# A build-time scheduler that charges DMA transposes and casting loads differently (sliding-window attention, then a multiplicative FFN)

## The chip, the cores and the metric

One core of one Trainium2 chip. The metric is device time in microseconds (us) of one execution; lower is better. The time of a kernel is the median of its runs.

## The reference, cut to what matters

```python
B, H, S, D = 4, 8, 768, 64          # q, k, v: float32
scores = matmul(q, k.T) / sqrt(D)
keep   = (key < 4) | ((0 <= row - key) & (row - key < 128))
a      = softmax(where(keep, scores, -1e9))
x      = (a @ v), heads side by side   # 3072 tokens x 512
h      = (x @ w1) * (x @ w2)           # 3072 x 1024
out    = (h @ w3) @ w_out              # 3072 x 512, float32
```

## The kernel before, in words

The work is done for four batches b = 0 to 3, each in two chunks c of 384 tokens. `w3 @ w_out` is folded into one matrix w3o at the start (transposes at L274, products at L299). For a batch, the keys and queries are loaded with a cast from float32 to bfloat16 (L152, issued by GpSimd, POOL), then brought into the transposed layout `qkT`. Batches 0 and 1 do that with TensorE (PE) transposes; batches 2 and 3 with **DMA transposes** issued by SyncE (SP) at L390, twelve for each batch: one for each of six blocks of 128 tokens and each of k and q. There are two homes of `qkT`; batch 2 reuses that of batch 0 and batch 3 that of batch 1.

Attention: scores at L467 (six visits of PE for a batch from batch 1 on), exp at L478 (ACT), masking at L484 (VectorE, DVE), the sink scores at L425 with their exp at L430, and the product with v at L536, normalized at L546 and L551 into `xs`. `xs` is transposed into `xT`, by PE at L572 and DVE at L576 for batches 0 and 1, by SP's DMA transposes at L592 for batches 2 and 3 (three for each chunk). The FFN takes a chunk of `xT`: 64 gate matmuls (L615), copies and products (L622, L630), then three output blocks of 8 matmuls each (L645), a copy (L652) and a store to `out` from SP (L658). A gate needs nothing but `xT` and weights, so FFN work of a chunk that is ready can fill PE while attention waits.

**What sets the order.** Every piece of work is an `Op` with an engine, a duration, the ops it depends on, a priority and the ring slots that it takes and frees. While the program is built, a planner simulates the engines: at each step it takes, over all engines, the op that starts earliest, emits its instructions and sets `o.done`, the time at which its readers may start. On PE, ACT, DVE and SP it takes the op that can start soonest; among those that can start at once, the lowest priority number (attention of batch b has 10b and some, the FFN 1000 and more). POOL takes its ops in the listed order. The planner's times exist only while the program is built; what remains is the order of instructions on each engine. On the chip an engine works through its instructions in that order, and one that waits for its data holds back all behind it.

Loads are charged to one shared DMA order `dma["at"]`: each adds its bytes over a rate and is due `LAND` after its turn. The transposes of L390 and L592 are charged 0.1 us of SP and are due 2.2 us later; the stores of L658 0.1 us and 2.0 us. None of these three touches the shared DMA order. The chunk's three `xT` transposes wait in the plan for one another (`evs[-1:]`).

```python
op.dma = nbytes * (1 + 96.0 / run) / 4.35e5
tp_of[s, kb] = Op(SP, 0.1, dmt, [got[n, b, kb]] + war, base, lat=2.2)
```

Of the kernel before, what the change touches and what calls it, by code (L numbers as in the profile page):

```python
# [21 lines left out]
def kernel(  # L22
# [23 lines left out]
    NP = H // 2  # L46
# [36 lines left out]
    for b in (2, 3):  # L83
        o = (b - 2) * 2 * NQ
# [35 lines left out]

    HOP = 0.12
    LAND = 1.9
    ops = []

    class Op:
# [21 lines left out]
    dma = dict(at=1.6)  # L147
# [41 lines left out]
    got = {}  # L189
# [138 lines left out]
    for b in range(B):  # L328
        kind = 0 if b == 0 else 1
        T = qkT_home[b % 2]  # L330
        war = []
# [50 lines left out]
        if b < 2:  # L382
            tdep = lambda c, r: [tp_of[c, r]] + ([tp_of[0, r]] if c else [])
        else:
            for kb in range(NB):
                for s, n, src in ((0, "k", kN), (1, "q", qN)):
                    got[n, b, kb] = load_nat(src, k if n == "k" else q, b, kb, fold_done)

                    def dmt(b=b, s=s, src=src, kb=kb, T=T):
                        nc.sync.dma_start_transpose(out=T[:, :, s, kb * P:(kb + 1) * P], in_=src[b][:, kb, :])  # L390
                    tp_of[s, kb] = Op(SP, 0.1, dmt, [got[n, b, kb]] + war, base, lat=2.2)
                got["v", b, kb] = load_v(b, kb)
            tdep = lambda c, r: [tp_of[s, kb] for s in range(2) for kb in range(3 * c + 3)]

# [165 lines left out]
        for c in range(NC):  # L560
            holder = [None]
            if b < 2:
                evs = []
                for n_h in range(2):
                    x = [holder]

                    def xtp(c=c, n_h=n_h, x=x, xs_first=xs_first):
                        tp = transposed(x[1].slot["mm"], 6 * P).rearrange("p (r j m) -> p r j m", r=2, m=P)
                        for i in range(2):
                            r = 2 * n_h + i  # L570
                            for j in range(QC):
                                nc.tensor.transpose(tp[:, i, j, :],  # L572
                                                    xs_first[c].slot["xs"][:, j, r * P:(r + 1) * P], ident[:])

                    def xtc(n_h=n_h, x=x):
                        nc.vector.tensor_copy(x[0][0].slot["xT"][:, 2 * n_h:2 * n_h + 2, :],  # L576
                                              transposed(x[1].slot["mm"], 6 * P).rearrange("p (r m) -> p r m", r=2))
                    a = Op(PE, cols(P, 6), xtp, [norm[c, 2 * n_h], norm[c, 2 * n_h + 1]], base + 2.5, takes=["mm"],
                           frees=[(xs_first[c], "xs")] if n_h else [])
                    x.append(a)  # L580
                    ev = Op(DVE, dve_us(6 * P, 2), xtc, [a] + ([holder[0]] if n_h else []), base + 2.5,
                            takes=["xT"] if n_h == 0 else [], frees=[(a, "mm")])
                    if n_h == 0:
                        holder[0] = ev
                    else:
                        a.deps.append(evs[0].deps[0])
                    evs.append(ev)
            else:
                evs = []
                for j in range(QC):  # L590
                    def xtd(c=c, j=j, holder=holder, xs_first=xs_first):
                        nc.sync.dma_start_transpose(out=holder[0].slot["xT"][:, :, j * P:(j + 1) * P],  # L592
                                                    in_=xs_first[c].slot["xs"][:, j, :])
                    ev = Op(SP, 0.1, xtd, [norm[c, r] for r in range(NP)] + evs[-1:], base + 2.5,
                            takes=["xT"] if j == 0 else [], lat=2.2,
                            frees=[(xs_first[c], "xs")] if j == QC - 1 else [])
                    if j == 0:
                        holder[0] = ev
                    evs.append(ev)
            chunk_dep[b, c] = (holder, evs)  # L600

    proj_ops = {}
    for b in range(B):
        for c in range(NC):
            holder, evs = chunk_dep[b, c]
            abh = [None]
            b_ops = []
            for dt in range(KFF):
                pr = 1000 + 200 * b + 100 * c + dt
                x = [holder]  # L610
                deps = evs + got["w", dt // 2]

                def gate(w_sb, dt, pg, holder=holder):
                    for kk in range(NP):
                        nc.tensor.matmul(pg[:, 0:TOK], w_sb[:, kk, dt * P:(dt + 1) * P],  # L615
                                         holder[0].slot["xT"][:, kk, :], start=(kk == 0), stop=(kk == NP - 1))
                y = []
                g1 = Op(PE, cols(TOK, 4), lambda g=gate, dt=dt, y=y: g(w1_sb, dt, y[0].slot["mm"]), deps, pr, takes=["mm"])
                y.append(g1)

                def acopy(y=y):
                    nc.scalar.copy(y[1].slot["a"][:], y[0].slot["mm"][:, 0:TOK])  # L622
                ac = Op(ACT, act_us(TOK), acopy, [g1], 0, takes=["a"], frees=[(g1, "mm")])
                y.append(ac)
                g2 = Op(PE, cols(TOK, 4), lambda g=gate, dt=dt, y=y: g(w2_sb, dt, y[2].slot["mm"]), deps + [g1], pr - 0.5,
                        takes=["mm"], frees=[(holder, "xT")] if dt == KFF - 1 else [])
                y.append(g2)

                def amul(dt=dt, y=y, abh=abh):
                    nc.vector.tensor_mul(abh[0].slot["ab"][:, dt, :], y[1].slot["a"][:], y[2].slot["mm"][:, 0:TOK])  # L630
                am_ = Op(DVE, dve_us(TOK), amul, [g2, ac] + ([abh[0]] if dt else []), 0, takes=["ab"] if dt == 0 else [],
                         frees=[(g2, "mm"), (ac, "a")])
                if dt == 0:
                    abh[0] = am_
                b_ops.append(am_)
            for mi in range(QC):
                m = QC * c + mi
                x = []
                last = b == B - 1 and m == NB - 1
                for n0, n1 in ([(0, 256), (256, 512)] if last else [(0, 512)]):  # L640
                    x = []

                    def proj(mi=mi, n0=n0, n1=n1, abh=abh, x=x):
                        for kk in range(KFF):
                            nc.tensor.matmul(x[0].slot["mm"][:, 0:n1 - n0], abh[0].slot["ab"][:, kk, mi * P:(mi + 1) * P],  # L645
                                             w3o[:, kk, n0:n1], start=(kk == 0), stop=(kk == KFF - 1))
                    p_ = Op(PE, cols(n1 - n0, 8), proj, b_ops + fold_done, 1150 + 200 * b + 100 * c + mi, takes=["mm"],
                            frees=[(abh, "ab")] if mi == QC - 1 and n1 == 512 else [])
                    x.append(p_)

                    def pcopy(n0=n0, n1=n1, x=x):
                        nc.scalar.copy(x[1].slot["o"][:, n0:n1], x[0].slot["mm"][:, 0:n1 - n0])  # L652
                    pc = Op(ACT, act_us(n1 - n0), pcopy, [p_], 0, takes=["o"], frees=[(p_, "mm")])
                    x.append(pc)

                    def pout(b=b, m=m, n0=n0, n1=n1, x=x):
                        t0 = b * S + m * P
                        nc.sync.dma_start(out=out[t0:t0 + P, n0:n1], in_=x[1].slot["o"][:, n0:n1])  # L658
                    Op(SP, 0.1, pout, [pc], 0, frees=[(pc, "o")], lat=2.0)


    free = {PE: 1.0, ACT: 2.2, DVE: 0.9, POOL: 0.9, SP: 0.8}
# [38 lines left out]
        return None if pick_ is None else (pick_[1], pick_[2])  # L701

    with tc.manual_schedule():
        left = len(ops)
        while left:
            moves = []
            for e in free:
                got_ = best(e)
                if got_:
                    moves.append((got_[0], e, got_[1]))  # L710
            start, e, o = min(moves, key=lambda x: (x[0], x[1]))
            if e == PE and start < 24.0 and start - free[PE] > 0.15:
                n = min(24, int((start - free[PE] - 0.1) / (cols(P) * (2 if free[PE] < WARM else 1))))
                sc = sc_home[0] if rings["sc"].free[0] == 0.0 else None
# [13 lines left out]
            us = o.us * (2 if e == PE and start < WARM else 1)  # L728
            free[e] = start + us
            o.done = start + us + o.lat  # L730
            if hasattr(o, "dma"):
                dma["at"] = max(dma["at"], start + us + (0.1 if e == POOL else 0.6)) + o.dma
                o.done = dma["at"] + LAND
            for h, n in o.frees:
                h = h[0] if isinstance(h, list) else h
                key = n
                ring = n[0] if isinstance(n, tuple) else n
                rings[ring].free[h.slot["#", key]] = o.done
# [37 lines left out]
```

## Time and profile before

| what | us |
|---|---|
| runs of the kernel | 231.79, 232.09, 232.44; median 232.09 |
| the profiled execution's own time | 231.57 |
| its span in the profile | 229.9 |
| PE busy in the span | 201.4 (88%) |
| DVE, ACT, POOL busy | 107.1, 100.2, 71.4 |
| PE's first instruction, end of its last | 1.06, 226.7 |

The span runs from the first instruction of the profiled execution to the last; its own time is 1.67 us longer. Busy time of PE counts a matmul for as long as it runs, so that matmuls at half the clock count double. "Idle before" in a row is the time for which the engine had nothing to run just ahead of that instruction, and the name behind the arrow is what ended it. SPq is the queue of SyncE, where DMA issues stand.

### The profile page before, as it was taken

To read this page: it belongs to the slowest core of one execution; us is meant where nothing else is said; L and a number is where in the kernel's file an instruction comes from. 1 tells how busy PE (TensorE), PEld (TensorE's weight loads), DVE (VectorE), ACT (ScalarE), POOL (GpSimd) and SP (SyncE) were. 2 spreads that over 40 slices of the span, in tenths; PEclk is the share of its full clock that TensorE was granted. 3 is DMA by queue.
4 is the path that set the end of the run, shared out by engine and by line. 5 is a ranking of instruction groups with operands and counts; after the bars stand their busy time and mean duration, and the time that the engine had idled before them with its cause. 6 is when DMAs were issued, how large, how long until landed. Compare 5 with 4: busy or idle time off the path is not lost.

```text
span 229.9 us, 4653 instructions
## 1 busy us (share of the span) xinstructions
PE 201.4 (88%) x1880; PEld 125.0 (54%) x1880; DVE 107.1 (47%) x249; ACT 100.2 (44%) x172; POOL 71.4 (31%) x93
## 2 busy tenths in 40 slices
PE   8999799968889953893089999999999999999994
PEld 8886465546546622362046656656555545546543
DVE  2424784568878852154037864773431312403300
ACT  3035554852377731375017667623323424334232
POOL 7846756699993556640000000000000000000000
PEclk9999999999999997589569999999999999999998
DMA  7999999999999999999910025203415012021033
GB/s 142 182 191 185 200 194 177 178 155 152 148 131 122 151 132 156 155 158 156 197 49 4 0 87 151 41 28 119 64 32 174 3 46 91 0 94 46 1 137 137
DMA packets 98437, 26.25 MB, mean 114 GB/s; under 512 B 88944, under 2 KB 94320, under 8 KB 98416
## 3 DMA queue, kind: packets, MB, share of 16 engines
q0 software_dynamic: 74944, 14.42, 81.0%
q1 hardware_dynamic: 23472, 11.54, 24.1%
q8 instruction: 14, 0.23, 0.4%
q14 instruction: 7, 0.06, 0.1%
HBM read 29.36 MB, written 6.29 MB: 155 GB/s over the span
## 4 chain that ended last, share of the span: by engine, by line
PE 55%; DMA 33%; POOL 6%; issue 2%; SPq 1%; ACT 0%; POOLq 0%; ACTq 0%
PE mm L615 30%; PE mm L645 17%; DMA qkT<-big 8%; DMA big<-in_k_dram 6%; DMA big<-in_moe_w_dram 5%; DMA early<-in_k_dram 5%; DMA w_sb<-in_moe_w_dram 4%; PE av L536 4%; DMA big<-in_moe_w_out_dram 3%; DMA vN<-in_v_dram 3%; PE sc L467 3%; POOL near L152 3%; POOL vN L152 1%; POOL big L152 1%; POOL w_sb L152 1%
## 5 line engine op out<-in xcount | busy, mean ns | idle before, releaser
L615 PE MATMUL mm<-xT,w_sb 128*128 128x384 bf16 x512 | 90.8, 329 | 0.1
L615 PEld LDWEIGHTS <-w_sb 128*128 128x128 bf16 x512 | 48.2, 98 | 35.0 <-issue 4.0
L630 DVE TENSOR_TENSOR ab<-a_sb,mm 128x384 bf16<-128x384 f32 x64 | 35.4, 553 | 60.4 <-PE mm L615 55.4
L478 ACT ACTIVATE ex<-sc 128x768 bf16<-128x768 f32 (+2 forms) x52 | 44.5, 896 | 16.6 <-PE sc L467 10.7
L622 ACT COPY a_sb<-mm 128x384 f32<-128x384 f32 x64 | 30.3, 480 | 37.1 <-PE mm L615 20.0
L645 PE MATMUL mm<-w3o,ab 128*128 128x512 bf16 (+1 forms) x200 | 46.3, 387 | 0.0
L645 PEld LDWEIGHTS <-ab 128*128 128x128 bf16 x200 | 19.5, 100 | 22.1 <-issue 3.4
L484 DVE TENSOR_TENSOR am<-ex,maskt 128x768 bf16<-128x768 bf16 (+2 forms) x52 | 30.2, 588 | 2.3 <-ACT ex L478 2.2
L652 ACT COPY o_sb<-mm 128x512 f32<-128x512 f32 (+1 forms) x25 | 14.2, 568 | 33.1 <-PE mm L645 33.1
L152 POOL DMA_DIRECT2D vN<-in_v_dram x24 | 21.2, 884 | 13.2 <-DMA big<-in_k_dram 8.2
L536 PEld LDWEIGHTS <-am 128*128 128x128 bf16 x352 | 18.2, 101 | 4.0 <-issue 1.0
L536 PE MATMUL av<-vN,am 128*128 128x65 bf16 x352 | 19.8, 198 | 0.0
L551 DVE TENSOR_TENSOR xs<-av,rec 128x384 bf16<-128x384 f32 x32 | 17.6, 551 | 0.2
L467 PE MATMUL sc<-qkT 64*128 64x256 bf16 (+1 forms) x248 | 15.0, 248 | 2.8 <-DMA qkT<-big 2.8
L299 PE MATMUL mm<-big,w3t 128*128 128x128 bf16 (+2 forms) x128 | 15.8, 273 | 0.6 <-DMA big<-in_moe_w_out_dram 0.6
L425 PE MATMUL mm<-qkT,ksbd 128*32 128x512 bf16 (+2 forms) x20 | 2.2, 432 | 15.3 <-DMA qkT<-big 14.7
L546 DVE RECIPROCAL rec<-av 128x6 f32<-128x6 f32 x32 | 6.2, 193 | 19.3 <-PE av L536 19.0
L303 ACT CAST w3o<-mm 128x128 bf16<-128x128 f32 (+2 forms) x16 | 5.9, 372 | 17.8 <-PE mm L299 17.7
L536 PE MATMUL av<-vsb,es 128*128 128x130 bf16 x64 | 13.5, 227 | 0.0
L467 PEld LDWEIGHTS <-qkT 64*128 64x128 bf16 x248 | 8.5, 97 | 8.6 <-issue 7.3
L299 PEld LDWEIGHTS <-w3t 128*128 128x128 bf16 x128 | 9.5, 98 | 4.5 <-issue 0.7
L152 POOL DMA_DIRECT2D big<-in_q_dram x12 | 10.6, 881 | 4.1 <-DMA vN<-in_v_dram 4.1
(52 smaller groups left out, 130.9 us busy)
## 6 DMA issues: line engine op xcount, KB each, us to landing
out_dram<-o_sb SPq DMA_DIRECT2D x23, 256.0 KB, 2.0
vN<-in_v_dram POOLq DMA_DIRECT2D x24, 128.0 KB, 10.1
w_sb<-in_moe_w_dram POOLq DMA_DIRECT2D x8, 256.0 KB, 9.7
big<-in_moe_w_dram POOLq DMA_DIRECT2D x7, 256.0 KB, 7.9
big<-in_k_dram POOLq DMA_DIRECT2D x12, 128.0 KB, 11.4
big<-in_q_dram POOLq DMA_DIRECT2D x12, 128.0 KB, 11.1
near<-in_k_dram POOLq DMA_DIRECT2D x6, 128.0 KB, 7.2
near<-in_q_dram POOLq DMA_DIRECT2D x6, 128.0 KB, 6.8
```

What stands on the lines that cost most here:

```text
L152: op = Op(eng, us, lambda: (nc.gpsimd if eng == POOL else nc.sync).dma_start(out=out, in_=in_), deps)
L299: nc.tensor.matmul(po, x[1].slot["w3t"][:, j, :], wo_sb[:, j, c0:c1], start=(j == 0), stop=(j == KFF - 1))
L467: nc.tensor.matmul(sc[:, e, c * P:(c + n) * P], T[hp, r, 0, kb * P:(kb + 1) * P], T[hp, r, 1, qb * P:(qb + n) * P], start=True, stop=True)
L478: nc.scalar.activation(y[1].slot["ex"][:, :, 0:w], y[0].slot["sc", i][:, :, 0:w], ACTF.Exp, scale=scale)
L484: nc.vector.tensor_mul(y[2].slot["am"][:, :, 0:w], y[1].slot["ex"][:, :, 0:w], maskt[:, :, m0:m0 + w].to_broadcast([P, 2, w]))
L536: nc.tensor.matmul(o, lhs, rhs, start=(i == 0), stop=(i == len(todo) - 1), skip_group_check=True)
L551: nc.vector.tensor_mul(xs_first[c].slot["xs"][:, :, r * P:(r + 1) * P].rearrange("p k (e d) -> p k e d", d=D), x[0].slot["av"][:, :, :, 0: ...
L615: nc.tensor.matmul(pg[:, 0:TOK], w_sb[:, kk, dt * P:(dt + 1) * P], holder[0].slot["xT"][:, kk, :], start=(kk == 0), stop=(kk == NP - 1))
L622: nc.scalar.copy(y[1].slot["a"][:], y[0].slot["mm"][:, 0:TOK])
L630: nc.vector.tensor_mul(abh[0].slot["ab"][:, dt, :], y[1].slot["a"][:], y[2].slot["mm"][:, 0:TOK])
L645: nc.tensor.matmul(x[0].slot["mm"][:, 0:n1 - n0], abh[0].slot["ab"][:, kk, mi * P:(mi + 1) * P], w3o[:, kk, n0:n1], start=(kk == 0), stop= ...
L652: nc.scalar.copy(x[1].slot["o"][:, n0:n1], x[0].slot["mm"][:, 0:n1 - n0])
```

## The change

The planner gets other costs; no op and no instruction is added or removed. A DMA transpose takes `TUS` = 1.25 us of SP, and its `turn`, also 1.25 us, of the shared DMA order. It is due 0.6 us after its start, plus its turn (twice that if the shared order is busy then), plus 1.3 us. A store keeps 0.1 us of SP and gets a turn of 0.7 us by the same formula. A POOL load may start only when the eighth load before it is due.

```diff
+    TUS = 1.25
...
-                    tp_of[s, kb] = Op(SP, 0.1, dmt, [got[n, b, kb]] + war, base, lat=2.2)
+                    tp_of[s, kb] = Op(SP, TUS, dmt, [got[n, b, kb]] + war, base)
+                    tp_of[s, kb].turn = TUS
...
-                    ev = Op(SP, 0.1, xtd, [norm[c, r] for r in range(NP)] + evs[-1:], base + 2.5,
-                            takes=["xT"] if j == 0 else [], lat=2.2,
+                    ev = Op(SP, TUS, xtd, [norm[c, r] for r in range(NP)] + evs[-1:], base + 2.5,
+                            takes=["xT"] if j == 0 else [],
                             frees=[(xs_first[c], "xs")] if j == QC - 1 else [])
+                    ev.turn = TUS
...
-                    Op(SP, 0.1, pout, [pc], 0, frees=[(pc, "o")], lat=2.0)
+                    Op(SP, 0.1, pout, [pc], 0, frees=[(pc, "o")]).turn = 0.7 * (n1 - n0) / 512
...
-        left = len(ops)
+        left, lanes = len(ops), []
...
             start, e, o = min(moves, key=lambda x: (x[0], x[1]))
+            if e == POOL and hasattr(o, "dma"):
+                if len(lanes) >= 8 and lanes[-8] > start:
+                    free[POOL] = lanes[-8]
+                    continue
...
             o.done = start + us + o.lat
+            if hasattr(o, "turn"):
+                busy = dma["at"] > start + 0.6
+                dma["at"] = max(dma["at"], start + 0.6) + o.turn
+                o.done = start + 0.6 + o.turn * (2 if busy else 1) + 1.3
             if hasattr(o, "dma"):
                 dma["at"] = max(dma["at"], start + us + (0.1 if e == POOL else 0.6)) + o.dma
                 o.done = dma["at"] + LAND
+                if e == POOL:
+                    lanes.append(o.done)
```

## Rows read from the trace of the kernel before

**Rows 1.** The page: busy shares, then PE, its clock and DMA in 40 slices.
```profile
PE 201.4 (88%) x1880; PEld 125.0 (54%) x1880; DVE 107.1 (47%) x249; ACT 100.2 (44%) x172; POOL 71.4 (31%) x93
...
PE   8999799968889953893089999999999999999994
...
PEclk9999999999999997589569999999999999999998
DMA  7999999999999999999910025203415012021033
```

**Rows 2.** Waits of PE, 80 to 120 us: who waited for whom, total us, times, longest.
```profile
PE mm L425 <- DMA qkT<-big: 14.7, 2, 10.4
PE sc L467 <- DMA qkT<-big: 2.8, 1, 2.8
```

**Rows 3.** Timeline of PE, 81 to 132 us: start, us, what, idle before.
```profile
81.13 0.39 PE L467 MATMUL sc<-qkT 64*128 64x256 bf16 x6
84.33 0.34 PE L467 MATMUL sc<-qkT 64*128 64x256 bf16 x4 [2.80 <-DMA qkT<-big]
84.60 2.89 PE L645 MATMUL mm<-w3o,ab 128*128 128x512 bf16 x8
...
92.79 0.62 PE L425 MATMUL mm<-qkT,ksbd 128*32 128x512 bf16 x4 [4.32 <-DMA qkT<-big]
...
115.81 0.62 PE L425 MATMUL mm<-qkT,ksbd 128*32 128x512 bf16 x4 [10.40 <-DMA qkT<-big]
...
131.87 1.90 PE L645 MATMUL mm<-w3o,ab 128*128 128x512 bf16 x8
```

**Rows 4.** PE by stretches: stretch, us, busy (count), granted clock, DMA share, GB/s.
```profile
84.33:88.47 4.14, 4.14 (x27) 0.62 1.92 155
92.79:98.40 5.61, 5.61 (x35) 0.50 1.89 156
98.40:101.00 2.60, 2.60 (x22) 0.88 1.98 153
115.81:119.90 4.09, 4.09 (x31) 0.55 0.00 0
120.00:160.00 40.00, 40.00 (x417) 1.00 0.20 56
```

**Rows 5.** The chain that ended last, 75 to 116 us: start, us, what.
```profile
75.56 8.73 DMA qkT<-big
...
85.72 6.94 DMA qkT<-big
...
98.13 12.98 DMA big<-in_k_dram
...
112.45 3.27 DMA qkT<-big
```

**Rows 6.** Timeline of PE, the end of the run.
```profile
160.34 9.26 PE L615 MATMUL mm<-xT,w_sb 128*128 128x384 bf16 x56
169.43 5.34 PE L645 MATMUL mm<-w3o,ab 128*128 128x512 bf16 x24
174.61 10.56 PE L615 MATMUL mm<-xT,w_sb 128*128 128x384 bf16 x64
```

**Rows 7.** The transposes of L390: ns min/median/max on SP's queue.
```profile
L390 SPq DMA_TRANSPOSE qkT<-big x24: 1188/1236/3111, 62.3 to 112.4; - x24
```

**Rows 8.** DMA issues: KB each (none given for transposes), median us to landing.
```profile
out_dram<-o_sb SPq DMA_DIRECT2D x23, 256.0 KB, 2.0
...
big<-in_k_dram POOLq DMA_DIRECT2D x12, 128.0 KB, 11.4
...
qkT<-big SPq DMA_TRANSPOSE x24, 7.2
...
xT<-xs SPq DMA_TRANSPOSE x12, 2.5
```

**Rows 9.** Timeline of POOL: first and last load for batches 2 and 3 (36 in all).
```profile
55.58 0.88 POOL L152 DMA_DIRECT2D big<-in_k_dram  x1
...
101.28 0.87 POOL L152 DMA_DIRECT2D vN<-in_v_dram  x1 [0.82 <-DMA big<-in_k_dram]
```

**Rows 10.** Timeline of SP's queue, 62 to 138 us.
```profile
62.33 36.58 SPq L390 DMA_TRANSPOSE qkT<-big  x18
99.00 0.53 SPq L658 DMA_DIRECT2D out_dram<-o_sb  x1
101.13 6.75 SPq L390 DMA_TRANSPOSE qkT<-big  x3
107.98 0.53 SPq L658 DMA_DIRECT2D out_dram<-o_sb  x1
108.60 5.06 SPq L390 DMA_TRANSPOSE qkT<-big  x3
113.76 21.34 SPq L658 DMA_DIRECT2D out_dram<-o_sb  x2
135.34 1.19 SPq L592 DMA_TRANSPOSE xT<-xs  x1
```

**Rows 11.** Timeline of DVE: last mask of batch 1, sink keys, last `xT` copies of batch 1.
```profile
82.25 0.68 DVE L484 TENSOR_TENSOR am<-ex,maskt 128x1024 bf16<-128x1024 bf16 x1
82.85 0.34 DVE L398 COPY ksbd<-qkT 64x16 bf16<-64x16 bf16 x2
...
101.49 0.56 DVE L576 COPY xT<-mm 128x768 bf16<-128x768 bf16 x1 [1.90 <-PE mm L572]
...
105.44 0.56 DVE L576 COPY xT<-mm 128x768 bf16<-128x768 bf16 x1 [0.31 <-PE mm L572]
```

## The prediction

> **What bounds the kernel now.** I began with the page's slices [rows 1]. PE is busy 201.4 us and every other engine about half of that or less, so PE is the bound, except where its row dips. The early dips and the last slice belong to the start and the final store. The dips that matter are in slices 15, 16 and 19 to 21 (80 to 92 us and 103 to 121 us), where the DMA row still reads 9 until loading ends near 115 us. Next I asked who PE waits for between 80 and 120 us: three waits, all for `qkT<-big`, the DMA transposes of batches 2 and 3, 14.7 + 2.8 = 17.5 us together [rows 2]. The timeline places them: 2.80 us in the middle of batch 2's first scores, 4.32 us at batch 2's sink scores, 10.40 us at batch 3's sink scores [rows 3]. The chain agrees: at these points it runs through transposes landing at 84.3, 92.7 and 115.7, and through the load ahead of the last of them [rows 5].
>
> The waits cost more than their length. After each of them PE works at 1.2 GHz for a while: granted 0.62, 0.50, 0.88 and 0.55 of full in the four stretches of work [rows 4]. A granted share g over t us means 2(1-g)t us at the lower level: 3.15 + 5.61 + 0.62 + 3.68 = 13.1 us. It can be seen in one instruction group: eight output matmuls take 2.89 us at 84.60 and 1.90 us at 131.87 [rows 3]. At full clock these 13.1 us of work take half, so 6.5 us are lost. From 120 to 160 us PE is busy throughout at 1.00 [rows 4]. So the recoverable sum is 17.5 + 6.5 = 24.0 us.
>
> Is there work to put there? Batch 1's two chunks of FFN are nearly all still to come at 105 us, and batch 0's output blocks too: the second half of `xT` for batch 1 is copied only at 101.49 and 105.44 [rows 11], because the last products of batch 1's attention stand in PE's order behind batch 2's scores and so behind the waits. The order is the fault, not a lack of work.
>
> **The change, part by part.** No instruction is added, so only the order can change. I work the code's formulas through POOL's and SP's lists; this tells when the planner believes data to be there, hence what stands ahead of what, and not what the chip will need.
>
> *Up to 58 us of the planner's time nothing moves.* POOL's list is fixed, and the limit of eight moves only issues: eight loads of batch 2 or 3 are 8 x 131072 x 2 x 1.375 / 435000 = 6.6 us of the shared order, more than the 2.9 us of issue and landing, so that order stays full and every due time as it was. The limit alone costs and brings nothing; it makes loads take their turn in the order among the transposes. The trace supports eight in flight: 36 loads start between 55.58 and 101.28, one in 1.31 us, and land 11.4 us after issue, 8.7 of them at a time [rows 8, 9].
>
> *The transposes of L390.* Charged now with 1.25 us of SP; the trace shows a median of 1.236 us on the queue [rows 7]. Landing is charged 3.15 us, or 4.4 behind a busy order, against a measured 7.2 and 3.27 us after the loads [rows 5, 8]. Three loads and two transposes then take 2.5 + 2.5 us of the order. Batch 2's last transpose is due at 84.0 instead of 74.0, batch 3's at 113.6 instead of 89.0. Measured: 92.7 and 115.7 [rows 5]. The new belief is 9 us too early for batch 2, and 2 us for batch 3.
>
> *Where PE then stands.* By its own costs the planner of before reached batch 2's scores at 77.2; the trace has them at 81.13 [rows 3], a lag of 3.9 us. In place of those scores PE now gets batch 0's three output blocks, 5.2 us [rows 6], and some 2 us of the last products and transposes of batch 1, which brings it to about 88.4 on the chip and past 84.0 in the plan. Then batch 2 comes again: one visit of scores whose transposes are there, a gate or none, then the sink scores or the next visit, which wait for the transpose landing at 92.7. I put PE there at 89.3, so **3.5 us of the batch 2 wait stay**; bounds 0 (several gates placed ahead) and 7.1 (both present waits). I add half a clock's loss after it: 6.2 us at the lower level were seen behind the 4.32 us wait (5.61 + 0.62), so 3.1 us; bounds 0 and 4.
>
> *Batch 3.* Planned from 113.7 on, on the chip 113.7 + 3.9 + 3.5 + 3.1 = 124, against transposes that landed at 115.7 [rows 5]. Between 84 and 113.7 the plan needs 30 us of work and has 2 x 15.6 of gates and output blocks for batch 1, 5.2 for batch 0's second chunk [rows 6] and some 7.5 of batch 2's attention, 44 us. So **the 10.40 us go, with the 3.7 us at the lower clock behind them**, and some 14 us are left to fill batch 3's attention. What is late next is SP's queue: six stores of batch 0 and batch 2's first `xT` transposes will stand among batch 3's last transposes, and each waits for PE. By the plan batch 3's last transpose starts at 109.2; with PE's lag of 10.5 us SP may reach it only at 119.7, and it lands 3.3 us later, at 123, one us before PE comes. Should that cover fail, the cost is the overshoot and a clock loss (rival B). The stores' bytes move into the time of loading, 0.7 us each by the plan and 0.53 us on the queue [rows 10]; 3 us more of DMA before batch 3's last landing, 119, is still ahead of 124.
>
> *The `xT` transposes and the stores.* `xT` is charged 3.15 to 4.4 us where 2.5 is measured [rows 8], in a chain of three, so batch 2's gates are planned up to 6 us late; the 14 us of batch 1's gates hide that, and without them it would be up to 6 us of idle PE. A store comes due after 2.6 to 3.3 us instead of 2.1 (measured 2.0 [rows 8]); three output buffers refilled every 1.73 us give 5.2 us, so nothing waits. Both: 0, bounds 0 and +6.
>
> *A rule that speaks against the charge.* In the rows a transpose holds SP for 1.236 us and a store of twice a load's bytes for 0.53 us, and batch 3's last transpose lands at 115.7 [rows 5, 7, 10]. The Trainium skill, Advanced Engine Details and Errata, section X-Bar Transpose (TRN2), says that transposing DMAs are as fast as plain ones, at 350 to 400 GB/s. By that, 128 KB take some 0.35 us (an estimate from that page), the planner's 1.25 us of shared order is 0.9 us too much for each of 24, and batch 3 would be due near 92, not 113.6. A planner with that figure would send PE to batch 3 some 21 us sooner and keep its wait; the landing at 115.7 sides with the larger charge, and the sum stays.
>
> **Sum**, against the profiled execution's 231.57: - 17.5 - 6.5 + 3.5 + 3.1 = 214.2. The median is 0.5 us above that execution, so 214.7.
>
> **The rivals.** *A: batch 2's wait goes as well.* For it: gates of batch 1 become ready just then and may stand ahead of the sink scores. Against: in the plan attention goes first wherever it can start at once, and it believes 84.0. 231.57 - 24.0 = 207.6, or 208 as a median.
>
> *B: SP becomes the bound for batch 3.* A store or an `xT` transpose, waiting for late PE, holds up batch 3's transposes; the covered margin is only 1 us. For it: in the rows a store already stands between batch 3's transposes, twice [rows 10]. At most the six last transposes wait for batch 2's first normalized chunk, near 118, and for three `xT` transposes and themselves, 9 x 1.25 us, then 3.3 us: 132.6, so 8.6 us of wait and some 3 us of clock: up to 226; its middle is 220.
>
> *C: slower, PE stays at 1.2 GHz.* After batch 2's remaining wait PE restarts at the lower level [rows 4] and would stay there if the new order of short gates and attention left small gaps all through batch 2's attention. The forecast already holds 3.1 us of this; it takes over at another 17.4 us lost, 41 us of run time at the lower level in all. Batch 2's stage, 30 us at full clock, would give 30 - 3.1 = 27 us: 241. Against: the clock was back within 6.2 us each time, and stretches of the same mixture run at 1.00 with no gap [rows 4].
>
> *D: the change does not do what it says.* Were batch 1's gates not ready when the waits come, PE's plan would idle there itself and both waits would stay: 229 to 233. Against: batch 1's last mask is done at 82.9, so what holds its `xT` is PE's order alone [rows 11].
>
> **How the numbers follow.** Forecast 0.62, A 0.12, B 0.14, C 0.06, D 0.06. The forecast's own range, from the bounds of the batch 2 wait and its clock, is 211 to 219; A stretches the range down to 208, B up to 223. Left outside are B's upper third, C, D and the edge of A, about 0.2. A measurement here can tell 0.3% from no change. Faster: forecast, A, B, 0.88; D within 0.3% or just above, 0.05; C and D's rest, 0.07.
>
> **What would show it.** Right: in the timeline of PE the output blocks of batch 0 at about 81 us instead of batch 2's scores; one wait for `qkT<-big` of 2 to 5 us ending near 92.7; none for batch 3, whose sink scores come near 124; granted clock 1.00 between 100 and 220; end of PE near 210. Wrong, by B: batch 3's sink scores waiting past 124, with SP's queue held by L658 or L592 before the last transposes. Wrong, by C: granted clock near 0.5 past 105 us. Wrong in size: batch 2's last transposes landing elsewhere than 92.7, as the stores now share the DMA engines then.

## The result, and the profile after

215.43 us median (214.61 to 215.81) against 232.00 of before: ratio 0.928, 95% interval 0.925 to 0.931. The forecast was 214.7. Below, the ratios are against before, and the one of run 7 leaves out one execution of 394.65 us, far from its other five. Line numbers move by one to three; sink scores are now L427, scores L469, gates L618, output blocks L648, stores L661, transposes L391 and L594.

The page of the changed kernel, the lines that answer to [rows 1]:

```profile
PE 196.4 (92%) x1880; PEld 122.4 (57%) x1880; DVE 108.2 (51%) x249; ACT 100.1 (47%) x172; POOL 71.1 (33%) x93
...
PE   8899699969879999559999999999999999999994
...
PEclk9999999999999999958999999999999999999999
DMA  7999999999999999999999453210163030030033
```

The dip in slices 19 to 21 is gone, and of the earlier one slices 17 and 18 are left. Waits of PE, 60 to 135 us, then its timeline, answering to [rows 2, 3]:

```profile
PE mm L427 <- DMA qkT<-big: 4.9, 1, 4.9
PE mm L407 <- DMA vN<-in_v_dram: 0.9, 1, 0.9
```

```profile
80.88 1.89 PE L648 MATMUL mm<-w3o,ab 128*128 128x512 bf16 x8
...
92.91 0.62 PE L427 MATMUL mm<-qkT,ksbd 128*32 128x512 bf16 x4 [4.90 <-DMA qkT<-big]
...
95.36 3.39 PE L618 MATMUL mm<-xT,w_sb 128*128 128x384 bf16 x12
...
118.96 8.61 PE L618 MATMUL mm<-xT,w_sb 128*128 128x384 bf16 x52
127.50 0.40 PE L427 MATMUL mm<-qkT,ksbd 128*32 128x512 bf16 x4
199.34 10.54 PE L648 MATMUL mm<-w3o,ab 128*128 128x512 bf16 x56
```

At 80.88, where batch 2's scores stood, PE now runs batch 0's first output block. Batch 2's sink scores still wait, 4.90 us, for a transpose that lands as late as before. Batch 3's come at 127.50 with no wait; 52 gate matmuls stand ahead of them in place of 10.40 us of nothing. PE by stretches (columns as in [rows 4]):

```profile
92.91:95.36 2.45, 2.45 (x21) 0.50 1.44 238
95.36:99.60 4.24, 4.24 (x36) 0.70 1.66 146
99.60:160.00 60.40, 60.40 (x579) 1.00 0.77 103
```

Half clock now covers 2.45 + 2 x 0.30 x 4.24 = 5.0 us, 2.5 us lost. So 4.9 + 2.5 = 7.4 us of the 24.0 are left and 16.6 are saved; the end of PE's last group moved by 16.8, from 226.7 to 209.9. The profiled execution took 215.81, 2.8 us beyond its span of 213.0, where before it was 1.7, so by its own time it gained only 15.8.

### The profile page after: what moved, and what is told of

It is laid out like the page before. It is cut to its first block, busy times and chain, and to the rows that moved or that the text cites. A ratio compares the mean times of both kernels' runs of the same rounds, so it can differ in the third digit from the quotient of the medians.

```text
span 213.0 us, 4649 instructions
## 1 busy us (share of the span) xinstructions
PE 196.4 (92%) x1880; PEld 122.4 (57%) x1880; DVE 108.2 (51%) x249; ACT 100.1 (47%) x172; POOL 71.1 (33%) x93
## 4 chain that ended last, share of the span: by engine, by line
PE 65%; DMA 25%; POOL 7%; issue 2%; ACT 0%; SPq 0%; POOLq 0%; ACTq 0%
PE mm L618 35%; PE mm L648 19%; DMA vN<-in_v_dram 8%; PE av L538 5%; DMA early<-in_k_dram 5%; DMA w_sb<-in_moe_w_dram 5%; PE sc L469 4%; DMA big<-in_moe_w_dram 4%; DMA qkT<-big 3%; POOL near L153 3%; POOL big L153 2%; POOL vN L153 1%; PE mm L574 1%; PE mm L427 1%; PE mm L407 0%
## 5 line engine op out<-in xcount | busy, mean ns | idle before, releaser
L618 PE MATMUL mm<-xT,w_sb 128*128 128x384 bf16 x512 | 91.6, 329 | 0.1
L618 PEld LDWEIGHTS <-w_sb 128*128 128x128 bf16 x512 | 48.0, 99 | 35.0 <-issue 4.4
L648 PE MATMUL mm<-w3o,ab 128*128 128x512 bf16 (+1 forms) x200 | 43.6, 370 | 0.0
L648 PEld LDWEIGHTS <-ab 128*128 128x128 bf16 x200 | 19.3, 98 | 20.4 <-issue 0.2
L538 PEld LDWEIGHTS <-am 128*128 128x128 bf16 x352 | 17.0, 97 | 3.2 <-issue 0.2
L538 PE MATMUL av<-vN,am 128*128 128x65 bf16 x352 | 18.8, 193 | 0.0
L469 PE MATMUL sc<-qkT 64*128 64x256 bf16 (+1 forms) x248 | 14.6, 245 | 0.0
L304 ACT CAST w3o<-mm 128x128 bf16<-128x128 f32 (+2 forms) x16 | 6.0, 372 | 16.9 <-PE mm L300 16.8
L538 PE MATMUL av<-vsb,es 128*128 128x130 bf16 x64 | 12.8, 219 | 0.0
L153 POOL DMA_DIRECT2D big<-in_k_dram x12 | 10.5, 879 | 4.9 <-DMA big<-in_q_dram 3.1
L469 PEld LDWEIGHTS <-qkT 64*128 64x128 bf16 x248 | 8.2, 96 | 6.2 <-issue 5.2
## 6 DMA issues: line engine op xcount, KB each, us to landing
big<-in_k_dram POOLq DMA_DIRECT2D x12, 128.0 KB, 11.1
```

The costliest lines, as they stand in the source:

```text
L153: op = Op(eng, us, lambda: (nc.gpsimd if eng == POOL else nc.sync).dma_start(out=out, in_=in_), deps)
L469: nc.tensor.matmul(sc[:, e, c * P:(c + n) * P], T[hp, r, 0, kb * P:(kb + 1) * P], T[hp, r, 1, qb * P:(qb + n) * P], start=True, stop=True)
L538: nc.tensor.matmul(o, lhs, rhs, start=(i == 0), stop=(i == len(todo) - 1), skip_group_check=True)
```

## The experiments

All edits are to the changed kernel. Where the planner alone is edited, the chip has the same instructions in another order.

**1. Without the charge of the L390 transposes.**

```diff
-tp_of[s, kb] = Op(SP, TUS, dmt, [got[n, b, kb]] + war, base)
-tp_of[s, kb].turn = TUS
+tp_of[s, kb] = Op(SP, 0.1, dmt, [got[n, b, kb]] + war, base, lat=2.2)
```

> The changed kernel with the charge of the L390 transposes put back to 0.1 us of SP and 2.2 us of landing; the limit of eight and the charges of the xT transposes and of the stores stay. Theory (the charge of the L390 transposes moves the order): the planner again believes batch 2 at 74.0 and batch 3 near 89, PE meets the same three waits of 2.8, 4.3 and 10.4 us, 232 us, within 1 of before. Rival (the limit and the other charges matter by themselves): a good part of the 16.6 us stays, 215 to 225.

232.82 us, ratio 1.005 (1.002 to 1.007). The timeline of its PE has the three waits back, at the same three places as [rows 3]:

```profile
84.33 0.34 PE L468 MATMUL sc<-qkT 64*128 64x256 bf16 x4 [2.52 <-DMA qkT<-big]
...
93.04 0.62 PE L426 MATMUL mm<-qkT,ksbd 128*32 128x512 bf16 x4 [5.99 <-DMA qkT<-big]
...
116.61 0.62 PE L426 MATMUL mm<-qkT,ksbd 128*32 128x512 bf16 x4 [11.87 <-DMA qkT<-big]
```

The limit and the other two charges alone bring nothing.

**2. That charge alone; 3. that charge and the limit.** Both take back the charges of `xT` (L594) and of the stores; the second run keeps the limit, the first has it off:

```diff
-if len(lanes) >= 8 and lanes[-8] > start:
+if False and lanes[-8] > start:
```

> Only the L390 transposes get the new charge; no limit of eight, old charges for xT transposes and stores. By the code's formulas the loads are then charged long before the transposes, so batch 2 is believed at 76.6 and batch 3 at 105.2. Theory: batch 2's waits stay as before (7.1 us and 4.7 us of clock loss), batch 3's 10.4 us and its 1.8 us of clock go: 219.5, between 218 and 221. Rival (the limit brings nothing): 215. Rival (nothing works without the limit): 232.

> The L390 charge and the limit of eight, old charges for xT transposes and stores. Theory: batch 2 believed at 84.0 as in the changed kernel, batch 3 at 113.5 instead of 115.9; one wait of 4.9 us at batch 2, none at batch 3: 215, within 1 of the changed kernel. Rival (the charges of xT and stores keep SP's queue in an order that feeds batch 3): a wait at batch 3 of 2 us or more, 218 to 224.

218.45 us (ratio 0.943, 0.940 to 0.946) and 215.25 (0.929, 0.925 to 0.933). Timelines of PE, first the charge alone, then with the limit:

```profile
83.67 0.50 PE L469 MATMUL sc<-qkT 64*128 64x256 bf16 x4 [2.57 <-DMA qkT<-big]
...
92.40 0.62 PE L427 MATMUL mm<-qkT,ksbd 128*32 128x512 bf16 x4 [4.41 <-DMA qkT<-big]
...
120.32 0.40 PE L427 MATMUL mm<-qkT,ksbd 128*32 128x512 bf16 x4
```

```profile
92.91 0.62 PE L427 MATMUL mm<-qkT,ksbd 128*32 128x512 bf16 x4 [4.68 <-DMA qkT<-big]
...
125.56 0.40 PE L427 MATMUL mm<-qkT,ksbd 128*32 128x512 bf16 x4 [0.30 <-DVE ab L632]
```

Read as a ladder: the transposes' charge removes batch 3's wait, 13.4 us in time; the limit, worth nothing in run 1, lets that charge move batch 2's due time as well, from 76.6 to 84.0 by the two expectations, and is worth another 3.2; the charges of `xT` and stores are worth nothing measurable (215.25 against 215.43).

**4. The turn of a plain transfer.**

```diff
-tp_of[s, kb].turn = TUS
+tp_of[s, kb].turn = 0.35
```

> The changed kernel with the turn of an L390 transpose in the shared DMA order cut from 1.25 to 0.35 us, the figure of a plain transfer of 128 KB at 350 to 400 GB/s; 1.25 us of SP stays. Batch 2 is then believed at 76.8, batch 3 at 96.3. Theory (the larger charge is right): batch 2's waits come back as before, PE reaches batch 3's sink scores near 112.4 and waits 3.3 us for the landing near 115.7: 223 to 225. Rival (transposes take no more of the DMA than plain transfers): data are there at 112 and earlier, no wait for batch 3, 219 or less.

228.21 us, ratio 0.982 (0.977 to 0.988). More than I expected; the rival falls, since the data were not there:

```profile
83.91 0.34 PE L469 MATMUL sc<-qkT 64*128 64x256 bf16 x4 [2.24 <-DMA qkT<-big]
...
92.88 0.62 PE L427 MATMUL mm<-qkT,ksbd 128*32 128x512 bf16 x4 [6.25 <-DMA qkT<-big]
...
118.36 0.62 PE L427 MATMUL mm<-qkT,ksbd 128*32 128x512 bf16 x4 [7.01 <-DMA qkT<-big]
```

PE was at batch 3 near 111.4, close to the 112.4 expected, but the last transpose landed at 118.3, not 115.7. The chain before that wait says why:

```profile
99.71 13.93 DMA big<-in_q_dram
113.64 0.02 issue
113.66 4.66 DMA qkT<-big
```

The last transpose was issued as soon as its load had landed, so no store held it in SP's queue; whether the stores' bytes slowed that load was not tried. For the order, 1.25 us is the better of the two charges. The run does not measure what a transpose takes of the DMA by itself, and a higher charge on the loads instead was not tried.

**5. Batch 2 due 8 us later in the plan.**

```diff
+tp_of[s, kb].more = 8.0 if b == 2 else 0.0
...
-o.done = start + 0.6 + o.turn * (2 if busy else 1) + 1.3
+o.done = start + 0.6 + o.turn * (2 if busy else 1) + 1.3 + getattr(o, "more", 0.0)
```

> The changed kernel with batch 2's L390 transposes due 8 us later in the plan; batch 2's sink scores are then planned at 92.5 instead of 84.1, batch 3's at 116.7. Theory (the remaining wait is only the planner's optimism, and work for PE is there): PE reaches batch 2 near 96.4, after the landing at 92.7, so no wait, no half clock: 4.9 + 2.5 us less than the changed kernel, 208. Batch 3 is reached near 120.6 against a landing of 119 or so. Rival B (SP's queue, where stores and xT transposes of batch 2 stand among batch 3's transposes, becomes the bound): a wait of 2 us or more for batch 3, 211 to 215. Rival (attention late, too little work left to fill it): gaps after 120, 213 or more.

214.04 us (0.921, 0.916 to 0.925): all waits for `qkT` are gone, and 1.4 us are gained instead of 7.4. A line of PE's timeline and two pieces of the chain say why:

```profile
93.85 8.88 PE L619 MATMUL mm<-xT,w_sb 128*128 128x384 bf16 x36 [3.56 <-ACT o_sb L656]
```

```profile
86.84 6.28 DMA out_dram<-o_sb
...
93.22 0.59 ACT o_sb L656
```

A fourth output block now follows the first three. Its copy needs one of three output buffers, all held by stores. The first block's copy was done at 83.4, but its store stood behind transposes in SP's queue until 86.84 and then took 6.28 us to land among the loads, not the 2.0 of [rows 8]. ACT stands, the PSUM slots that it should empty stay full, PE waits 3.56 us, and works at 0.71 of the clock from 93.85 to 104. Neither rival named this. The view of `o_sb` from 78 to 100 us has all four stores slow:

```profile
DMA to landing us min/median/max: 6.3/6.8/7.8
```

**6. Matmuls on zeros in the remaining wait.**

```diff
 def ss(b=b, q0=q0, w=w, T=T, x=x):
+    for i in range(80 if b == 2 else 0):
+        nc.tensor.matmul(x[0].slot["mm"][:, 0:P], zeros[:], zeros[:], start=True, stop=True)
```

> The changed kernel, same order, with 80 matmuls on zeros put into PE's queue ahead of batch 2's sink scores, 4.5 us at full clock, into a PSUM slot that is overwritten; the results are not touched. It separates the wait from the clock. Theory: the wait is filled, data still land at 92.7, and the granted clock stays at 1.00 from 93 to 100 us, so the 2.5 us lost to the lower clock come back: 212.9. Rival (the clock loss counted is not real time, other engines set the pace of batch 2): 215.4, no change. Rival (the dummies run past the landing or hold a slot that others need): 216 or more.

212.30 us (0.914, 0.911 to 0.917), 3.1 less than the changed kernel; the spans of the two profiled executions, 213.0 and 210.6, differ by 2.4. Timeline and stretches of PE:

```profile
88.23 4.63 PE L427 MATMUL mm<-zeros 128*128 128x128 bf16 x80
92.79 0.40 PE L429 MATMUL mm<-qkT,ksbd 128*32 128x512 bf16 x4
```

```profile
92.60:95.36 2.76, 2.76 (x34) 1.00 1.53 204
95.36:99.60 4.24, 4.24 (x51) 1.00 1.52 181
```

Batch 2's last transpose is issued at 85.9 and lands 6.8 us later, at 92.7, as before; what differs is the clock, 1.00 where 0.50 and 0.70 stood. The clock's share of the loss is real time and can be had apart from the wait.

**7 and 8. Values loaded last,** then also batch 2 due 5 us later (as in run 5):

```diff
+            for kb in range(NB):
                 got["v", b, kb] = load_v(b, kb)
```

> The changed kernel with the six value loads of batches 2 and 3 moved behind all twelve key and query loads of their batch in POOL's list. Batch 2 is then believed at 76.9, its sink scores planned at 78.1, so PE is there at 82.0. Theory (batch 2's landing is set by the loads ahead of it, 1.31 us each): batch 2's last transpose lands 6 x 1.31 = 7.9 us sooner, at 84.8; wait 2.8 us instead of 4.9, about 213. Rival (the landing is set by the transposes themselves): it stays at 92.7, the wait grows to 10 us and the time to 221.

> As the run before (values last) with batch 2's transposes due 5 us later, so that its sink scores are planned at 82.8 and reached at 86.6. Theory: data are there at 84.8, no wait at batch 2; batch 3 planned at 109.6, reached at 113.5 against a landing near 108 to 112: 207.5 to 208.5, level with the run that only delays batch 2. Rival (loads and transposes of batch 3 do not come sooner, since the same bytes have to be moved): a wait of 2 to 5 us for batch 3, 211 to 216.

217.43 us (0.934, 0.930 to 0.938) and 216.54 (0.931, 0.926 to 0.935): neither better than the changed kernel, and the second not clear of it. The chain of the first and its waits of PE, 60 to 130 us:

```profile
81.85 7.42 DMA qkT<-big
```

```profile
PE mm L428 <- DMA qkT<-big: 6.2, 1, 6.2
PE mm L408 <- DMA vN<-in_v_dram: 2.1, 1, 2.1
```

Batch 2's last transpose landed at 89.3, 3.4 us sooner and not 7.9, so the loads ahead of it are less than half of its delay as I had costed it. In the rest the transposes queue by themselves: the last load that they need starts at 65.31 and lands after 11.1 us, at 76.4, while the last three are issued from 77.4 to 81.9 and take 7.4 to 8.6 us each. The first value block came later and PE waited 2.1 us for it, in front of the sinks' values. With the later due time, batch 3 waited:

```profile
119.77 0.62 PE L429 MATMUL mm<-qkT,ksbd 128*32 128x512 bf16 x4 [2.85 <-DMA qkT<-big]
```

**9. Run 5 with five output buffers; 10. the same, 6 us later instead of 8.** The two float32 staging tiles of the start are free by then:

```diff
-o=o_home
+o=o_home + stage
```

> The run in which batch 2's transposes are due 8 us later, with the same order of PE's instructions, but five output buffers instead of three: the two staging tiles of the start join the ring. Theory (the 3.6 us wait of that run is the store's landing of 6.3 us while loads are in flight, which three output buffers do not cover): no wait of PE for o_sb, none for qkT, no half clock between 80 and 130 us, 208, within 1. Rival (the order itself has gaps, the output buffer was only the last to come): another wait of 2 us or more takes its place, 211 to 215.

> The same with five output buffers and batch 2's transposes due 6 us later instead of 8: sink scores planned at 90.6, reached at 94.5 against a landing at 92.7. Theory: the same 208; how much later does not matter once it is past the landing and work is there. Rival (the landing scatters by more than 1.8 us from run to run): a wait in some runs, their times spread over 2 us or more.

208.94 us (0.900, 0.897 to 0.903) and 209.83 (0.904, 0.901 to 0.906). PE's order in run 9 is that of run 5, so the 5.1 us between them are the output buffers. In both profiles what is left is a short wait at batch 3; run 9's line, and the chain ahead of it:

```profile
122.20 0.40 PE L428 MATMUL mm<-qkT,ksbd 128*32 128x512 bf16 x4 [1.38 <-DMA qkT<-big]
```

```profile
104.08 14.65 DMA big<-in_q_dram
118.73 0.02 issue
118.74 3.32 DMA qkT<-big
```

Here too the last transpose waits for its load and not for SP's queue.

**11. Run 9 with batch 3 due 4 us later too** (`else 4.0`).

> Five output buffers, batch 2's transposes due 8 us later and batch 3's 4 us later: batch 3's sink scores planned at 122.0 instead of 116.7, reached near 126 against a landing that was 122.2 with five buffers. Theory (the 1.4 us wait left there is again only the planner's optimism, SP's queue holding batch 3's last transposes): no wait for qkT at all, 1.4 us less than with five buffers alone, 207.5. Rival (SP's queue moves along with PE, so that the transposes are issued later too): the wait stays, 209. Rival (work to fill runs out): gaps in PE between 100 and 122 us, 210 or more.

207.93 us, ratio 0.896 (0.893 to 0.899), the fastest version here by its median, 7.5 us below the changed kernel; its interval overlaps that of run 9. No wait for `qkT` is left, and no half clock from 80 to 130 us (columns as in [rows 4]):

```profile
127.07 0.40 PE L428 MATMUL mm<-qkT,ksbd 128*32 128x512 bf16 x4
```

```profile
80.00:130.00 50.00, 49.88 (x469) 1.00 1.55 154
```

## Why the prediction was right, point by point

**The recoverable sum** of 24.0 us was borne out: run 11, with no wait and no half clock there, is 24.1 us below the 232.00 of before.

**Batch 3's wait gone:** right, and by the step named. Run 2 shows that the transposes' own charge does it.

**What stays of batch 2's wait:** 3.5 us forecast, 4.90 measured. The step said that a visit of scores, and perhaps a gate, would come before the sink scores, with PE there at 89.3. The sink scores came first and PE stood there at 88.0. The clock after it was put at 3.1 us and measured 2.5. Together 7.4 against 6.6, which is about the 0.7 by which the forecast was low. That it is so little is in part luck: the wait was put 1.4 us too short and the clock's loss 0.6 too long.

**SP's queue at batch 3:** I put its last transposes one us ahead of PE, at 123 against 124. SP's queue of the changed kernel, answering to [rows 10]:

```profile
117.55 1.22 SPq L391 DMA_TRANSPOSE qkT<-big  x1
118.88 2.29 SPq L594 DMA_TRANSPOSE xT<-xs  x1
121.25 0.53 SPq L661 DMA_DIRECT2D out_dram<-o_sb  x1
121.89 1.23 SPq L594 DMA_TRANSPOSE xT<-xs  x1
123.21 2.53 SPq L391 DMA_TRANSPOSE qkT<-big  x2
```

Stores and `xT` transposes do stand in between, and the last two are issued only at 123.2 and 124.5; they land 2.4 us after issue, the last at 127.0, half a us before PE. PE came at 127.50, later than forecast, in part because those same stores and transposes delay batch 3 in the plan as well, due at 115.9 by the expectation of run 3 and not at 113.6: without their charges (run 3) PE comes at 125.56. The forecast gave that cover one us, and it held by half a us. Rival B did not occur: the 0.9 and 1.4 us of runs 9 and 10 are a wait for batch 3 too, but run 9's chain has a load behind it and not a store or an `xT` transpose in SP's queue.

**The limit alone** costs and brings nothing: right by run 1. I did not price it with the transposes, where it is 3.2 us of the gain.

**The stores at nothing** was wrong as a step, though it cost nothing here. Three buffers, refilled every 1.73 us, were set against a landing of 2.0, a median mostly of stores behind the loads. Run 5 shows 6.28 among the loads, after 3.5 us more in SP's queue. The trace of before had it already: its three stores issued from 99.0 to 113.8 landed after 7.5, 6.2 and 2.5 us. In the changed kernel only three output blocks come before batch 2, so batch 2's wait covers it; once that cover goes, it is 5.1 us (runs 5 and 9).

**The rule on transposes** (the Trainium skill, Advanced Engine Details and Errata, X-Bar Transpose (TRN2)) would have a transpose cost what a plain transfer does. Run 4 disagrees as far as a planner goes: charged so, 12.8 us of the 16.6 are lost again. What a transpose takes of the DMA stays open: at the 153 to 156 GB/s of [rows 4], loads and transposes mixed, 128 KB take 0.85 us (an estimate), between the two charges.

**Rivals A, C and D** did not occur. A's time, 208 as a median, was reached only in run 11, after two more due times and two more buffers.

## What to carry to other kernels

When an order is fixed at build time, compare for each batch when the planner believes data to be there with when the trace shows them landing: each optimistic due time becomes a wait in an in-order queue, and the clock's loss comes on top. Charge a shared queue with the transfers that crowd it, at durations measured while it is full (here the transposes counted, while the charges of `xT` and stores changed nothing measurable); a cost or a limit that does nothing alone can be what lets another one work. After each repaired due time, look for the next: here batch 3's transposes, then batch 2's, then the stores' buffers, then batch 3's again.

## What the runs showed of the hardware that was not expected

A store of 256 KB takes 6.28 us to land among loads in flight (run 5), against a median of 2.1 over the changed kernel's whole run.

POOL's loads are never more than eight in flight. Counted from issue and landing in each of the 13 traces, 74 to 76 of the 84 loads, of 128 to 512 KB, are the eighth when they are issued and none is a ninth. The limit of eight in the plan is what the traces show.

A wait of some 2.5 us at the same place in batch 2's scores was followed by full clock in some profiles and by a fall in others. After 2.80 us PE fell to 0.62 [rows 3, 4], and after 2.57 in run 2 to 0.61; after 2.52 in run 1 and 2.24 in run 4 it stayed at 1.00. Runs 2, 1 and 4:

```profile
83.67:88.00 4.33, 4.10 (x26) 0.61 1.95 155
```

```profile
84.33:88.00 3.67, 2.66 (x26) 1.00 1.86 154
```

```profile
83.91:88.00 4.09, 2.66 (x26) 1.00 1.92 155
```

The two longer waits are those with a fall; four profiles do not show whether length alone decides.
